# Moving one operand of VectorE's bit operations into PSUM, and lo parts to GpSimd, in the first group of a chain of attention and two expert layers

## The chip, the cores and the metric

One Trainium2 chip, one core of it. The metric is the device time of one execution in microseconds (us). Five engines work side by side: TensorE (PE, with its weight loads as PEld), VectorE (DVE), ScalarE (ACT), GpSimd (POOL) and SyncE (SP), which only issues transfers here.

## What is computed

```python
def _attn_ref(q, k, v, g_norm):                       # 4 x 8 x 576 x 64
    kv = np.einsum('bhsd,bhse->bhde', k, v)
    out = np.einsum('bhsd,bhde->bhse', q, kv)
    rms = np.sqrt(np.mean(out * out, axis=-1, keepdims=True) + 1e-06)
    return (out / rms * g_norm).astype(np.float32)

def _moe_ref(x, w_in, w_out):                         # 2304 x 512, d_ff 2048
    h = x @ w_in
    relu6 = np.clip(h + 3.0, 0.0, 6.0)
    g = h * relu6 / 6.0
    return (g @ w_out).astype(np.float32)
```

A third layer sends each of the 2304 tokens to one of 8 experts (softmax gate, a capacity of 576 per expert), with two products and a ReLU, and weights the result by the gate. `w_in` and `w_out` come as float64, all else as float32.

## The kernel before

TensorE multiplies in float16. Every float32 operand x is split into a hi part, float16(x), and a lo part, float16(x - hi), and a product is three matmuls: hi by hi, hi by lo, lo by hi (`PAIRS`). The float64 weights are first turned into float32 by bit operations on their two 32-bit words.

The 2304 tokens are worked in five groups of 512 (the last has 256). For a group, `mm1` makes 16 blocks of h (f = 0 to 15, twelve matmuls of 512 columns each), `gated` turns each block of h into hi and lo of g, and `mm2` sums g by `w_out` into four PSUM banks. The attention of a batch of 576 tokens, which makes the group's input `x0T`, runs between. The experts come last, with weights that are loaded and split meanwhile.

What matters here is the first group, where the weights are converted while they are first used. It is written out by hand, in program order on every engine (`early`, a manual schedule):

- `load_kv(0)`, `gn` (two transfers for `g_norm`), `load_q(0)`, three pieces of `w_in`, `load_kv(1)` and `wg_raw` (the gate's weights, L150) are issued on SyncE's one queue in this order. L178 (ScalarE) and L179 (VectorE) make hi and lo of `wg`; their place in the engines' order is the scheduler's.
- `first_group` makes q times kv for 512 tokens into four PSUM banks `o`, squares them on ScalarE, copies them to SBUF on VectorE (`oc`, L347), sums the squares by a matmul (`ss`), and makes 1/rms by a square root, a reciprocal and one Newton step (L361 to L366). A matmul by `back` spreads it over the rows (`spread`); `norm` multiplies (L383) and copies the hi part on ScalarE (L384); `low` subtracts for the lo part (L388).
- `f64_piece` converts a piece of 128 x 1024 weights: three bit operations on VectorE (L228, L231, L234), two scaled copies on ScalarE (L239 the hi part, L241 the float32 in place), and the lo part on GpSimd (L243). `convert(i, 3)` runs three of these steps. At every even f the loop runs the three VectorE steps of the piece two ahead, then the other three of the next piece. There are 8 pieces of `w_in` and 8 of `w_out`; the second product's loop goes on in the same manner with pieces 10 to 15. A raw piece has one of three buffers, and `feed` issues the next load behind L234.
- `gated` has L570 (ScalarE), L572 (VectorE, one operand from SBUF and one from PSUM), L574 (ScalarE) and L575, the lo part, on GpSimd, but on VectorE for every fourth f.
- `att_o(1, (3, 1, 1))` makes the attention rows of batch 1 inside the second product's loop, 3, 1 and 1 blocks at a time: squares (L429), sums (L430), the norm (L435 to L452), the product (L458), then `hand_over` (hi L470 on ScalarE, lo L472 on GpSimd, a transposing DMA into x0T). Its `row` tiles have two buffers.

PSUM has eight banks: `psb` holds seven tiles of one bank, `pss` one tile for the gate (`lg`, `pos`, `cp`). `warm` issues matmuls whose result nobody reads.

```python
            eng.tensor_tensor(out=gt[:, 1, :n_t], in0=g6, in1=gt[:, 0, :n_t], op=ALU.subtract)   # L575
...
            gated(0, f, hs[f], nc.vector if f % 4 == 3 else nc.gpsimd)                           # L659
```

Of the kernel before, what the change touches and what calls it, by code (L numbers as in the profile page):

```python
# [30 lines left out]
def moe_chain(ctx: ExitStack, tc: tile.TileContext, qT, k, v, g_norm, w_in, w_out,  # L31
# [150 lines left out]
    nc.vector.tensor_scalar(out=gn, in0=gn, scalar1=S_WIN, scalar2=None, op0=ALU.mult)  # L182
# [88 lines left out]
    with ExitStack() as p1:  # L271
        psb = p1.enter_context(tc.tile_pool(name="psb", bufs=7, space=bass.MemoryType.PSUM))
# [7 lines left out]

        x0T = {}
# [6 lines left out]
        def att_kv(b):  # L288
# [28 lines left out]
        def first_group(w_a, w_b):  # L317
# [16 lines left out]
            nc.vector.tensor_scalar(out=back, in0=head, scalar1=mine, scalar2=None, op0=ALU.is_equal)  # L334
# [618 lines left out]
```

## Time and profile before

| | us |
|---|---|
| median of 3 runs | 728.54 (726.21 to 728.97) |
| the profiled execution | 726.38 |
| its span, first to last instruction | 724.6 |
| TensorE busy | 663.7 (92% of the span) |
| VectorE busy | 356.1 (49%) |
| ScalarE busy | 276.4 (38%) |
| GpSimd busy | 112.2 (15%) |
| mean granted TensorE clock | 0.966 |

The profile counts an instruction as busy from its start to its end, a wait for a shared resource inside it too. An instruction's row has its start, its duration, its line, its tiles (out<-in), its shape, and in brackets the idle time of its engine before it with what ended it. The group of the expert layer is the longest part; the first group ends when the second group's first matmul starts.

### The profile page before, as it was taken

To read this page: it belongs to the slowest core of one execution; us is meant where nothing else is said; L and a number is where in the kernel's file an instruction comes from. 1 tells how busy PE (TensorE), PEld (TensorE's weight loads), DVE (VectorE), ACT (ScalarE), POOL (GpSimd) and SP (SyncE) were. 2 spreads that over 40 slices of the span, in tenths; PEclk is the share of its full clock that TensorE was granted. 3 is DMA by queue.
4 is the path that set the end of the run, shared out by engine and by line. 5 is a ranking of instruction groups with operands and counts; after the bars stand their busy time and mean duration, and the time that the engine had idled before them with its cause. 6 is when DMAs were issued, how large, how long until landed. Compare 5 with 4: busy or idle time off the path is not lost. (4 is left out here: it accounts for less than half of the span.)

```text
span 724.6 us, 12556 instructions
## 1 busy us (share of the span) xinstructions
PE 663.7 (92%) x5049; PEld 378.7 (52%) x5049; DVE 356.1 (49%) x790; ACT 276.4 (38%) x428; POOL 112.2 (15%) x107
## 2 busy tenths in 40 slices
PE   7876969699989999999999999988999999996995
PEld 3332424244454444554444448655776776674754
DVE  1888875745666145461465027552124661163353
ACT  1356553334552035530254007431134551254252
POOL 1145653440100010000000001001111011000101
PEclk7899998989999999999999999999999999998999
DMA  8869669543164760634100015618819995099650
GB/s 307 281 204 280 186 184 350 172 121 118 51 154 83 214 210 19 232 61 107 44 31 1 14 44 133 174 31 132 218 39 298 287 235 161 31 266 195 208 104 23
DMA packets 125221, 108.78 MB, mean 150 GB/s; under 512 B 83943, under 2 KB 88551, under 8 KB 125152
## 3 DMA queue, kind: packets, MB, share of 16 engines
q1 hardware_dynamic: 122096, 98.42, 50.9%
q0 software_dynamic: 3056, 9.41, 3.8%
q8 instruction: 47, 0.77, 0.5%
q14 instruction: 22, 0.18, 0.1%
HBM read 64.55 MB, written 25.23 MB: 124 GB/s over the span
## 5 line engine op out<-in xcount | busy, mean ns | idle before, releaser
L590 PE MATMUL x<-w,g 128*128 128x512 f16 x864 | 197.5, 388 | 14.0 <-POOL w L243 10.6
L562 PE MATMUL h<-x0T,w 128*128 128x512 f16 (+1 forms) x960 | 196.8, 363 | 12.5 <-POOL w L243 10.6
L562 PEld LDWEIGHTS <-w 128*128 128x128 f16 x960 | 92.4, 99 | 106.9 <-POOL w L243 13.0
L590 PEld LDWEIGHTS <-g 128*128 128x128 f16 x864 | 84.5, 99 | 117.2 <-issue 24.4
L849 PE MATMUL h<-xe,w 128*128 128x128 f16 (+1 forms) x1920 | 109.3, 220 | 13.2 <-PEq L887 5.3
L849 PEld LDWEIGHTS <-w 128*128 128x128 f16 x1920 | 106.9, 100 | 20.1 <-issue 14.5
L864 PE MATMUL y<-w,ht 128*128 128x512 f16 (+1 forms) x504 | 112.3, 379 | 1.6 <-DVE ht L773 1.6
L864 PEld LDWEIGHTS <-ht 128*128 128x128 f16 (+1 forms) x504 | 48.9, 99 | 55.7 <-issue 1.7
L854 DVE SCALAR_TENSOR_TENSOR ht<-h,ht 128x512 f16<-128x512 f32 (+1 forms) x40 | 26.5, 663 | 93.0 <-ACT ht L853 89.4
L572 DVE SCALAR_TENSOR_TENSOR g<-t,h 128x512 f32<-128x512 f32 (+1 forms) x80 | 50.1, 630 | 39.4 <-ACT t L570 39.4
L574 ACT ACTIVATE g<-g 128x512 f16<-128x512 f32 (+1 forms) x80 | 46.2, 584 | 54.5 <-DVE g L572 54.2
L570 ACT ACTIVATE t<-h,b 128x512 f32<-128x512 f32 (+1 forms) x80 | 51.2, 641 | 37.6 <-PE h L562 37.5
L543 POOL DMA_INDIRECT xd<-row,sl x18 | 19.6, 1091 | 283.2 <-DVE sl L541 162.1
L575 DVE TENSOR_TENSOR g<-g,g 128x512 f16<-128x512 f32 (+1 forms) x68 | 42.1, 627 | 29.7 <-ACT g L574 29.7
L259 DVE SCALAR_TENSOR_TENSOR w<-raw_kv,w 128x1024 f16<-128x1024 f32 x33 | 40.1, 1220 | 32.1 <-ACT w L256 31.2
L875 POOL DMA_INDIRECT out<-ysb,ti x21 | 21.2, 1011 | 208.3 <-ACT ysb L874 87.4
L597 DVE SCALAR_TENSOR_TENSOR row<-x,row 128x512 f16<-128x512 f32 x18 | 12.3, 690 | 75.6 <-ACT row L596 75.6
L243 POOL TENSOR_TENSOR w<-f,w 128x1024 f16<-128x1024 f32 x16 | 40.3, 2516 | 55.9 <-ACT f L241 55.6
L853 ACT ACTIVATE ht<-h 128x512 f16<-128x512 f32 (+1 forms) x40 | 23.0, 576 | 64.6 <-PE h L849 45.7
L874 ACT ACTIVATE ysb<-y,meta 128x512 f32<-128x512 f32 (+1 forms) x21 | 14.4, 687 | 76.4 <-PE y L864 55.7
L596 ACT ACTIVATE row<-x 128x512 f16<-128x512 f32 x18 | 10.8, 597 | 76.5 <-PE x L590 37.8
L256 ACT ACTIVATE w<-raw_kv 128x1024 f16<-128x1024 f32 x33 | 34.4, 1047 | 0.9 <-ACTq L887 0.8
(121 smaller groups left out, 474.3 us busy)
## 6 DMA issues: line engine op xcount, KB each, us to landing
raw_kv<-in_w SPq DMA_DIRECT2D x33, 512.0 KB, 6.2
xd<-zero SPq DMA_DIRECT2D x20, 514.0 KB, 8.1
raw_w<-in_w SPq DMA_DIRECT2D x19, 512.0 KB, 6.9
raw_w<-in_w_in SPq DMA_DIRECT2D x8, 1024.0 KB, 5.9
raw_w<-in_w_out SPq DMA_DIRECT2D x8, 1024.0 KB, 9.9
raw_q<-in_w SPq DMA_DIRECT2D x12, 512.0 KB, 5.2
raw_q<-in_qT SPq DMA_DIRECT2D x8, 576.0 KB, 5.8
out<-zero SPq DMA_DIRECT2D x6, 768.0 KB, 4.0
```

What stands on the lines that cost most here:

```text
L243: nc.gpsimd.tensor_tensor(out=d[:, 1], in0=f32, in1=d[:, 0], op=ALU.subtract)
L256: nc.scalar.activation(d[:, :, 0, :], r, AF.Copy, scale=scale)
L259: nc.vector.scalar_tensor_tensor(out=d[:, :, 1, :], in0=r, scalar=scale, in1=d[:, :, 0, :], op0=ALU.mult, op1=ALU.subtract)
L562: nc.tensor.matmul(ps, w[:, a, c * 256 + o : c * 256 + o + P], x0T[g][:, b * NP + c, :n_t], start=start and n == 0, stop=stop and n == len ...
L570: nc.scalar.activation(t, ps, AF.Relu, bias=b3, scale=sc / (S_X0 * S_WIN))
L572: nc.vector.scalar_tensor_tensor(out=g6, in0=t, scalar=6.0 * sc, in1=ps, op0=ALU.min, op1=ALU.mult)
L574: nc.scalar.activation(gt[:, 0, :n_t], g6, AF.Copy)
L575: eng.tensor_tensor(out=gt[:, 1, :n_t], in0=g6, in1=gt[:, 0, :n_t], op=ALU.subtract)
L590: nc.tensor.matmul(ps, gts[g][f][:, a, j * P : (j + 1) * P], w[:, b, o : o + DM], start=(f == 0 and i == 0), stop=(f == NF - 1 and i == le ...
L849: nc.tensor.matmul(ps[:, f, :ns], w[c // 2][:, c % 2, a, f * P : (f + 1) * P], xe[:, b * NP + c, :ns], start=(n == 0), stop=(n == 3 * NP - 1))
L854: nc.vector.scalar_tensor_tensor(out=ht[:, 1, :, :ns], in0=ps[:, :, :ns], scalar=0.0, in1=ht[:, 0, :, :ns], op0=ALU.max, op1=ALU.subtract)
L864: nc.tensor.matmul(ps[:ns], hts[q][:, a, f, :ns], w[f // 2][:, f % 2, b, :], start=(n == 0), stop=(n == 3 * NFE - 1))
```

## The change

- The bit operations keep their intermediate `u` in PSUM (L228 and L231 write it, L231 and L234 read it): a tile of two banks, which the gate's `lg`, `pos` and `cp` now share. `psb` has six banks.
- In the norm, the products with `ms` are kept in the second half of the bank `ss`; the factor -0.5 goes into `back`.
- The copies `oc` of q times kv go from VectorE to ScalarE, behind the square root and the first piece's two copies. The first piece's three bit operations stand ahead of the norm.
- `gated` of the first group sends every lo part to GpSimd, and `low(3)` goes there too. The pieces 1 and 2 are converted behind all of `norm`.
- Eight warm-up matmuls go between the second and the third chunk of `att_kv(0)`, fourteen more ahead of the sixteen behind the norm. `load_q(0)` is issued ahead of `gn`.
- `att_o(1)` works in parts of (2, 1, 1, 1), from f = 4 on.

```diff
     load_kv(0)
+    load_q(0)
     gn = const.tile([P, 1], F32, name="gn")
...
-    load_q(0)
...
+            u = two_banks("u").bitcast(I32).rearrange("p (c n) -> p c n", c=c)
             t = cvt.tile([P, c, n], I32, tag="f", name="f")
-            nc.vector.tensor_scalar(out=t, in0=r[:, :, :, 1], scalar1=3, scalar2=0x3FFFFFFF,
+            nc.vector.tensor_scalar(out=u, in0=r[:, :, :, 1], scalar1=3, scalar2=0x3FFFFFFF,
                                     op0=ALU.logical_shift_left, op1=ALU.bitwise_and)
             yield
-            nc.vector.scalar_tensor_tensor(out=t, in0=r[:, :, :, 1], scalar=-0x40000000, in1=t,
+            nc.vector.scalar_tensor_tensor(out=u, in0=r[:, :, :, 1], scalar=-0x40000000, in1=u,
                                            op0=ALU.bitwise_and, op1=ALU.bitwise_or)
             yield
-            nc.vector.scalar_tensor_tensor(out=t, in0=r[:, :, :, 0], scalar=29, in1=t,
+            nc.vector.scalar_tensor_tensor(out=t, in0=r[:, :, :, 0], scalar=29, in1=u,
                                            op0=ALU.logical_shift_right, op1=ALU.bitwise_or)
...
-        psb = p1.enter_context(tc.tile_pool(name="psb", bufs=7, space=bass.MemoryType.PSUM))
+        psb = p1.enter_context(tc.tile_pool(name="psb", bufs=6, space=bass.MemoryType.PSUM))
...
+        def two_banks(name):
+            return pss.tile([P, 1024], F32, tag="s", name=name)
...
+                if pause and c == 2:
+                    pause()
...
-            nc.vector.tensor_scalar(out=back, in0=head, scalar1=mine, scalar2=None, op0=ALU.is_equal)
+            nc.vector.tensor_scalar(out=back, in0=head, scalar1=mine, scalar2=-0.5 * S_X0,
+                                    op0=ALU.is_equal, op1=ALU.mult)
...
-                oc = sg.tile([P, T], F32, tag="g", name="oc")
-                nc.vector.tensor_copy(oc, ps)
-                banks.append(oc)
+                banks.append(ps)
...
-                if p:
-                    next(w_a)
+            for _ in range(3):
+                next(w_a)
...
+            for p in range(NP):
+                oc = sg.tile([P, T], F32, tag="g", name="oc")
+                nc.scalar.activation(oc, banks[p], AF.Copy)
+                banks[p] = oc
...
-            nc.vector.tensor_tensor(out=u, in0=r, in1=r, op=ALU.mult)
-            nc.vector.scalar_tensor_tensor(out=u, in0=u, scalar=-0.5 * S_X0, in1=ms, op0=ALU.mult, op1=ALU.mult)
-            nc.vector.scalar_tensor_tensor(out=r, in0=u, scalar=1.5 * S_X0, in1=r, op0=ALU.add, op1=ALU.mult)
+            nc.vector.tensor_tensor(out=q, in0=r, in1=ms, op=ALU.mult)
+            nc.vector.tensor_tensor(out=q, in0=r, in1=q, op=ALU.mult)
+            nc.vector.scalar_tensor_tensor(out=r, in0=q, scalar=-3.0, in1=r, op0=ALU.add, op1=ALU.mult)
+            warm(14)
             warm(16)
...
-            next(w_b)
             x3 = norm(3)
             low(2, x2, nc.vector)
-            low(3, x3, nc.vector)
-            next(w_b)
-            next(w_b)
+            low(3, x3, nc.gpsimd)
+            for _ in range(3):
+                next(w_b)
...
-        warm(11)
-        keep_kv(att_kv(0))
+        wb = bank("warm")
+        warm(11, wb)
+        keep_kv(att_kv(0, lambda: warm(8, wb)))
...
-            gated(0, f, hs[f], nc.vector if f % 4 == 3 else nc.gpsimd)
+            gated(0, f, hs[f], nc.gpsimd)
...
-        att1 = att_o(1, (3, 1, 1))
+        att1 = att_o(1, (2, 1, 1, 1))
...
-            if 5 <= f <= 11:
+            if 4 <= f <= 11:
                 next(att1)
```

The order moves at three places that matter. ScalarE ahead of the first group's first matmul: `w` and `f` are a weight piece, `x0T` the group's input, `wg` the gate's weights. Before:

```order
L358 ACTIVATE rms<-ss,eps 128x256
L239 ACTIVATE w<-f,gn 128x1024
L241 ACTIVATE f<-f,gn 128x1024
L384 ACTIVATE x0T<-xn 128x512 x4
L178 ACTIVATE wg<-wg_raw 128x4x8
L239 ACTIVATE w<-f,gn 128x1024
```

and now:

```order
L363 ACTIVATE rms<-ss,eps 128x256
L239 ACTIVATE w<-f,gn 128x1024
L241 ACTIVATE f<-f,gn 128x1024
L368 ACTIVATE oc<-o 128x512 x4
L178 ACTIVATE wg<-wg_raw 128x4x8
L395 ACTIVATE x0T<-xn 128x512 x4
L239 ACTIVATE w<-f,gn 128x1024
```

The four `oc` copies came in, and L178 went from behind the four copies into x0T to ahead of them.

VectorE in the norm, up to the second tile. Before:

```order
L361 TENSOR_SCALAR rms<-ss 128x256
L363 RECIPROCAL rms<-rms 128x256
L364 TENSOR_TENSOR rms<-rms 128x256
L365 SCALAR_TENSOR_TENSOR rms<-rms 128x256
L366 SCALAR_TENSOR_TENSOR rms<-rms 128x256
L383 TENSOR_TENSOR xn<-oc,r 128x256 x4
L388 TENSOR_TENSOR x0T<-xn,x0T 128x512
```

and now:

```order
L371 TENSOR_SCALAR ss<-ss 128x256
L372 RECIPROCAL rms<-rms 128x256
L374 TENSOR_TENSOR ss<-rms,ss 128x256
L375 TENSOR_TENSOR ss<-rms,ss 128x256
L376 SCALAR_TENSOR_TENSOR rms<-ss,rms 128x256
L394 TENSOR_TENSOR xn<-oc,r 128x256 x2
L179 SCALAR_TENSOR_TENSOR wg<-wg_raw,wg 128x4x8
L394 TENSOR_TENSOR xn<-oc,r 128x256 x2
L399 TENSOR_TENSOR x0T<-xn,x0T 128x512
```

The products write `ss`, which is in PSUM, and L179 stands between the first and the second tile.

GpSimd in the first product's rounds (L243 a weight piece, L575 the lo part of g). Before:

```order
L243 TENSOR_TENSOR w<-f,w 128x1024
L575 TENSOR_TENSOR g<-g_415,g 128x512
L243 TENSOR_TENSOR w<-f,w 128x1024
L575 TENSOR_TENSOR g<-g_464,g 128x512
L575 TENSOR_TENSOR g<-g_484,g 128x512
```

and now:

```order
L243 TENSOR_TENSOR w<-f,w 128x1024
L585 TENSOR_TENSOR g<-g_442,g 128x512
L585 TENSOR_TENSOR g<-g_462,g 128x512
L243 TENSOR_TENSOR w<-f,w 128x1024
L585 TENSOR_TENSOR g<-g_492,g 128x512
L585 TENSOR_TENSOR g<-g_512,g 128x512
```

Every round has two lo parts there; before it was two and one in turn.

## Rows read from the trace of the kernel before

**Rows 1.** Busy us (x instructions) by stretch, then clock, DMA share, GB/s
```profile
core 0: us, PE busy (x) PEld busy (x) DVE busy (x) ACT busy (x) POOL busy (x), PEclk, DMA share, GB/s
31.80:164.05 132.25, 105.05 (x514) 47.60 (x513) 95.26 (x108) 63.26 (x86) 64.20 (x36) 0.90 0.69 208
164.05:724.60 560.55, 534.94 (x4391) 318.74 (x4389) 246.95 (x657) 205.41 (x332) 42.89 (x54) 0.99 0.50 126
```

**Rows 2.** TensorE in order of time: start, us, what, [idle before, releaser]
```profile
109.99 13.10 PE L590 MATMUL x<-w,g 128*128 128x512 f16 x47 [3.76 <-POOL w L243]
...
141.09 0.38 PE L590 MATMUL x<-w,g 128*128 128x512 f16 x1 [3.07 <-ACT w L239]
144.38 4.85 PE L590 MATMUL x<-w,g 128*128 128x512 f16 x11 [2.91 <-POOL w L243]
...
164.05 20.88 PE L562 MATMUL h<-x0T,w 128*128 128x512 f16 x96
```

**Rows 3.** VectorE and ScalarE in one round of the first product
```profile
60.66 0.67 ACT L570 ACTIVATE t<-h,b 128x512 f32<-128x512 f32 x1
...
61.37 0.69 DVE L572 SCALAR_TENSOR_TENSOR g<-t,h 128x512 f32<-128x512 f32 x1 [1.27 <-ACT t L570]
...
62.63 1.13 ACT L239 ACTIVATE w<-f,gn 128x1024 f16<-128x1024 f32 x1
62.70 1.22 DVE L231 SCALAR_TENSOR_TENSOR f<-raw_w,f 128x1024 int32<-128x1024 int32 x1
...
63.85 1.15 ACT L241 ACTIVATE f<-f,gn 128x1024 f32<-128x1024 f32 x1
63.95 2.06 DVE L234 SCALAR_TENSOR_TENSOR f<-raw_w,f 128x1024 int32<-128x1024 int32 x1
64.91 0.67 ACT L570 ACTIVATE t<-h,b 128x512 f32<-128x512 f32 x1
...
65.94 0.67 DVE L572 SCALAR_TENSOR_TENSOR g<-t,h 128x512 f32<-128x512 f32 x1
...
67.96 0.69 DVE L572 SCALAR_TENSOR_TENSOR g<-t,h 128x512 f32<-128x512 f32 x1 [1.34 <-ACT t L570]
```

**Rows 4.** VectorE's groups from 40 to 97 us: busy us, mean ns | idle
```profile
L234 DVE SCALAR_TENSOR_TENSOR f<-raw_w,f 128x1024 int32<-128x1024 int32 x8 | 19.5, 2442 | 0.3
...
L572 DVE SCALAR_TENSOR_TENSOR g<-t,h 128x512 f32<-128x512 f32 x15 | 10.2, 681 | 9.1 <-ACT t L570 9.1
L228 DVE TENSOR_SCALAR f<-raw_w 128x1024 int32<-128x1024 int32 x7 | 5.3, 757 | 0.0
L575 DVE TENSOR_TENSOR g<-g,g 128x512 f16<-128x512 f32 x3 | 2.1, 692 | 2.1 <-ACT g L574 2.1
```

**Rows 5.** VectorE beside GpSimd, in order of time
```profile
26.18 2.12 POOL L243 TENSOR_TENSOR w<-f,w 128x1024 f16<-128x1024 f32 x1 [22.29 <-ACT f L241]
26.22 2.36 DVE L365 SCALAR_TENSOR_TENSOR rms<-rms 128x256 f32<-128x256 f32 x1
...
41.06 2.66 POOL L243 TENSOR_TENSOR w<-f,w 128x1024 f16<-128x1024 f32 x1 [7.43 <-ACT f L241]
41.66 0.68 DVE L572 SCALAR_TENSOR_TENSOR g<-t,h 128x512 f32<-128x512 f32 x1
```

**Rows 6.** ScalarE's L570 of f = 2 and of f = 14
```profile
47.84 0.69 ACT L570 ACTIVATE t<-h,b 128x512 f32<-128x512 f32 x1 [0.65 <-PE h L562]
...
95.66 0.67 ACT L570 ACTIVATE t<-h,b 128x512 f32<-128x512 f32 x1
```

**Rows 7.** The transfers of the microsecond from 27 to 28
```profile
DMA packets 542, 0.19 MB, mean 188 GB/s; under 512 B 457, under 2 KB 457, under 8 KB 542
```

**Rows 8.** The first copy into x0T, and the third matmul of f = 2
```profile
31.11 1.29 ACT L384 ACTIVATE x0T<-xn 128x512 f16<-128x512 f32 x2 [5.01 <-DVE xn L383]
...
43.78 1.71 PE L562 MATMUL h<-x0T,w 128*128 128x512 f16 x4 [3.32 <-POOL w L243]
```

**Rows 9.** The second group's x after its q products, and the products' release
```profile
217.71 26.07 PE L590 MATMUL x<-w,g 128*128 128x512 f16 x120
...
220.89 1.29 DVE L458 TENSOR_TENSOR xs<-o,r 128x512 f32<-128x512 f32 x2
```

More of the change, by code (lines that the diff above doesn't have):

```diff
@@ L181, in moe_chain @@
     xd = dram.tile([E * CAPP, ROW], F16, name="xd")
-    nc.vector.tensor_scalar(out=gn, in0=gn, scalar1=S_WIN, scalar2=None, op0=ALU.mult)
     steps = []
@@ L286, in group_tile, with att_kv @@
             return x0T[g]
-        def att_kv(b):
+        def att_kv(b, pause=None):
             ps = bank("kv").rearrange("p (a b) -> p a b", b=P)
@@ L338, in first_group @@
             banks = []
-            ss = bank("ss")[:, : T // 2]
             sqs = []
@@ L345, in first_group @@
                 nc.scalar.activation(sq, ps, AF.Square)
-                oc = sg.tile([P, T], F32, tag="g", name="oc")
-                nc.vector.tensor_copy(oc, ps)
-                banks.append(oc)
+                banks.append(ps)
                 sqs.append(sq)
-                if p:
-                    next(w_a)
+            for _ in range(3):
+                next(w_a)
+            ss = bank("ss")
             for p, sq in enumerate(sqs):
                 for i, rows in enumerate(halves):
-                    nc.tensor.matmul(ss[rows, :], sel[:, p, :], sq[:, i * T // 2 : (i + 1) * T // 2],
+                    nc.tensor.matmul(ss[rows, : T // 2], sel[:, p, :], sq[:, i * T // 2 : (i + 1) * T // 2],
                                      start=p == 0, stop=p == NP - 1)
-            small = [sg.tile([P, 2, T // 2], F32, tag="g", name="rms") for _ in range(2)]
-            ms, r, u = small[0][:, 0], small[0][:, 1], small[1][:, 0]
-            nc.scalar.activation(u, ss, AF.Sqrt, bias=eps, scale=1.0 / D)
+            ms, q = ss[:, : T // 2], ss[:, T // 2 :]
+            r = sg.tile([P, T // 2], F32, tag="g", name="rms")
+            u = sg.tile([P, T // 2], F32, tag="g", name="rms")
+            nc.scalar.activation(u, ms, AF.Sqrt, bias=eps, scale=1.0 / D)
             next(w_a)
             next(w_a)
-            nc.vector.tensor_scalar(out=ms, in0=ss, scalar1=1.0 / D, scalar2=1.0e-6, op0=ALU.mult, op1=ALU.add)
+            for p in range(NP):
+                oc = sg.tile([P, T], F32, tag="g", name="oc")
+                nc.scalar.activation(oc, banks[p], AF.Copy)
+                banks[p] = oc
             next(w_a)
+            nc.vector.tensor_scalar(out=ms, in0=ms, scalar1=1.0 / D, scalar2=1.0e-6, op0=ALU.mult, op1=ALU.add)
             nc.vector.reciprocal(r, u)
-            nc.vector.tensor_tensor(out=u, in0=r, in1=r, op=ALU.mult)
-            nc.vector.scalar_tensor_tensor(out=u, in0=u, scalar=-0.5 * S_X0, in1=ms, op0=ALU.mult, op1=ALU.mult)
-            nc.vector.scalar_tensor_tensor(out=r, in0=u, scalar=1.5 * S_X0, in1=r, op0=ALU.add, op1=ALU.mult)
+            nc.vector.tensor_tensor(out=q, in0=r, in1=ms, op=ALU.mult)
+            nc.vector.tensor_tensor(out=q, in0=r, in1=q, op=ALU.mult)
+            nc.vector.scalar_tensor_tensor(out=r, in0=q, scalar=-3.0, in1=r, op0=ALU.add, op1=ALU.mult)
+            warm(14)
             warm(16)
@@ L487, in gate_block @@
                 nc.sync.dma_start_transpose(xT, row[:, : 2 * DM])
-            lg = pss.tile([P, P], F32, tag="s", name="lg")
+            lg = two_banks("lg")
             for a in range(2):
@@ L504, in gate_block @@
             yield
-            pos = pss.tile([P, P], F32, tag="s", name="pos")
+            pos = two_banks("pos")
             nc.tensor.matmul(pos[:, :E], upper, oh, start=True, stop=False)
@@ L602, in moe_chain @@
         for i in range(NS):
-            w, c = f64_piece(("i", i), gn)
+            w, c = f64_piece(("i", i), gn, two_banks)
             win.append(w)
@@ L606, in moe_chain @@
         for i in range(NS):
-            w, c = f64_piece(("o", i), S_WOUT)
+            w, c = f64_piece(("o", i), S_WOUT, two_banks)
             wout.append(w)
@@ L629, in moe_chain, with warm @@
         early.enter_context(tc.manual_schedule())
-        def warm(n):
-            ps = bank("warm")
+        def warm(n, ps=None):
+            ps = bank("warm") if ps is None else ps
             for _ in range(n):
@@ L637, in moe_chain @@
         next(start)
-        warm(11)
-        keep_kv(att_kv(0))
+        wb = bank("warm")
+        warm(11, wb)
+        keep_kv(att_kv(0, lambda: warm(8, wb)))
+        nc.vector.tensor_scalar(out=gn, in0=gn, scalar1=S_WIN, scalar2=None, op0=ALU.mult)
         hs = next(start)
@@ L734, in moe_chain @@
         mm2(ps, g, 0, range(4, 6))
-        cp = pss.tile([P, P], F32, tag="s", name="cp")
+        cp = two_banks("cp")
         nc.tensor.matmul(cp[:, :E], ones, total, start=True, stop=True)
```

2 lines of the change are left out of this document (1 added, 1 removed).

## The prediction

> **What bounds the kernel now.** I read the busy time by stretch first [rows 1], then TensorE's order of time [rows 2], one round of the first group on VectorE and ScalarE [rows 3], and last the rows that price single steps. The stretches split the run in two. From 164.05 us on TensorE works 534.94 of 560.55 us: it is the bound, and nothing that the change does to other engines shows there. Before that, from the first group's first matmul at 31.80 us, it works 105.05 of 132.25 us at a mean granted clock of 0.90, while VectorE works 95.26: the 27.2 us that TensorE stands idle are what the change can reach. The order of time names whom TensorE waits for: GpSimd's lo part of a weight piece (L243), or the ScalarE copy before it (L239) [rows 2].
>
> A round of the group's first product handles two f. VectorE's and ScalarE's rows hang on each other [rows 3]: VectorE's L572 (61.37), then ScalarE's L239 (62.63), L241 (63.85), L570 (64.91), and on VectorE's side L228, L231 (62.70) and L234 (63.95) before the next L572 (65.94) and the one behind it (67.96). The reader is to see L234: 2.06 us, where L231 of the same shape took 1.22. Over the stretch L234 means 2442 ns [rows 4]. The cause shows at 26 us: GpSimd's L243 ran from 26.18 to 28.30, and VectorE's L365, which has a quarter of L231's elements, took 2.36 us from 26.22 on: it ended just behind L243 [rows 5]. But L572, with one operand from PSUM, ran 0.68 us at 41.66, inside an L243 that lasted from 41.06 to 43.72 [rows 5]. So it is two SBUF operands on VectorE that collide with GpSimd, and the change puts one of them in PSUM.
>
> **The rounds of the first product.** Six rounds lie between the L570 of f = 2 (47.84) and that of f = 14 (95.66) [rows 6]: 47.82 / 6 = 7.97 us each. What is the round without collisions?
> - By ScalarE [rows 3]: from L572 at 61.37 to L239 1.26, to L241 1.22, to L570 1.06, from an L570 to its L572 0.71 (60.66 to 61.37), and from one L572 of a pair to the other 2.02: 6.27 us.
> - By VectorE: from L572 to L231 1.33 (62.70 - 61.37), to L234 1.25, L234 itself 1.22, and 2.02: 5.82, to which the dearer L228 is added. No row has a VectorE write into PSUM. L228 is bounded below by the 0.69 that it takes undisturbed (757 ns on the mean [rows 4]) and above by twice L231, 2.44. I take 1.22: with an operand in PSUM it becomes like L572 and L231, which pass one element a cycle (512 in 0.68, 1024 in 1.22). That adds 0.53: 6.35 us.
> - By GpSimd: an L243, which took 2.66 at its longest in rows 5, and two L575 of half its elements are about 5.3.
> - By TensorE: 24 matmuls at 20.88 / 96 = 0.2175 [rows 2] are 5.2 us.
>
> VectorE's 6.35 ends last, just ahead of ScalarE. The gain is 7.97 - 6.35 = 1.62 a round, **9.7 us** over six. The 692 ns of L575 that leave VectorE in every second round [rows 4] are in it. If L228 stayed at 0.69, ScalarE's 6.27 would set the round and the gain be 10.2; if it took 2.44, the round would be 7.57 and the gain 2.4.
>
> [...]
>
> **The start.** The change takes four copies off VectorE, frees L365 from its 2.36 us, keeps TensorE at work before the third chunk of `att_kv` and lets q go ahead of `g_norm`. My reckoning has the norm ready some 4 us sooner, the 30 warm-up matmuls done at about 24.9, and VectorE's first normalised tile ready at 26.7. But ScalarE's queue now has L178 (`wg`) ahead of the four copies into x0T, where it stood behind them, and L179 stands on VectorE ahead of the second tile. `wg_raw` is loaded behind nearly everything else of the start, and the same bytes lie before it as now. Its 512 packets of 32 bytes pass between 27 and 28 us: 457 small ones in that microsecond [rows 7]. So L178 can't run before 28; I take 29.7, between that and 31.11, where the copies start now [rows 8]. The first copy into x0T then moves from 31.11 to 29.9 only: **1.2 us**. From there to the third matmul of f = 2 (43.78) it is 12.67 us now [rows 8]; GpSimd takes one lo part off VectorE (0.69) and L243 takes 2.12 instead of 2.66 (0.54), the late L179 costs 0.35: about 0.9 more. Conversion 2 and two round trips on VectorE end 0.6 us behind that, so I count **1.5 us** at the L570 of f = 2. Bounds: nothing, if `wg_raw` lands at 31; 4.5, if it lands before 26.7.
>
> **Between the two products.** From 95.66 to the second matmul of f = 2 of the second product (109.99) it is 14.33 us. L243 of that piece falls from about 2.66 to 2.12 (0.5), and the last pair of f, cleared of its collision, is shorter by 0.6: **1.1 us**. TensorE's idle time there (3.76) [rows 2] stays.
>
> **The second product, 109.99 to 164.05.** It loses 3.07 us to L239 and 2.91 to L243 near 141 [rows 2]: `att_o(1)`'s first part has three rows where there are two row buffers, the third waits for a transposing DMA, and the conversion stands behind it on ScalarE. Parts of (2, 1, 1, 1) don't need a third. Behind the gap 11 matmuls take 4.85 us, 0.44 each where 0.2175 is the full rate: 2.4 more. Together 8.4. Laying the queues out anew, piece by piece, I get short waits instead, at f = 8, 10, 12 and 14, of which 0.6 is net new: **7.8 us**. Between nothing, if the new waits are as long, and 10.
>
> **The sum.** 1.5 + 9.7 + 1.1 + 7.8 = 20.1 us. Behind 164.05 every engine's order is unchanged and TensorE is the bound, so all of it should reach the end. The bank that is taken from `psb` I cost at nothing: the second block of a later group would take the first q product's bank, given back at 222.2 (220.89 + 1.29), and it starts 48 matmuls, 10.4 us, behind 217.71 [rows 9]; without that cover it would cost some 3 us in each of two groups. From the profiled execution's 726.38 us (724.6 of it span) that leaves 706.3. The median of the runs is 728.54, 2.2 above; I say 707.0, between 706.3 and 708.4.
>
> **Rivals.**
> - GpSimd and VectorE still exclude each other, so the change doesn't do what it says. For it: no row shows a VectorE write to PSUM. Against it: L572 at 41.66 [rows 5]. L575 leaves VectorE and the parts of `att_o(1)` still help: 1.5 + 4 + 0.5 + 4 = 10 us, some **716 us**. A lost bank that does cost 6 us comes out near it, at 712. Chance 0.18.
> - `wg_raw` lands before ScalarE comes to L178. Against it: the packets at 27 us [rows 7]. The start then gains 3 us more: **703.5 us**. Chance 0.13.
> - Slower: VectorE's writes into PSUM are slow. The round tips past 7.97 when L228 and L231 need over 2.03 us each (6.35 + 2 x 0.81). At 2.44 the round is 8.8: six rounds lose 5 us, two conversions in the start 2.4 each, and the second product keeps no gain: 726.4 + 5 + 4.8 - 2.6 (start and tail), some **734 us**. [...] Chance 0.03.
>
> **How the numbers follow.** The forecast has 0.64, 702 to 711; with 0.18, 0.13 and 0.03 that leaves 0.02 for no change (waits that only move, 725 to 730). The range 699 to 717 takes in the second rival whole and most of the first. A measurement of this kernel tells about 0.5% from no change, 3.6 us: faster 0.95, same 0.02, slower 0.03.
>
> **What would show it.** L228 and L234 near 1.22 in the rounds, L243 at 2.1 to 2.2 throughout; L580 (L570 before) every two f at 6.3 us; L178 on ScalarE waiting for a DMA until about 29.7, with TensorE idle before its first h; no gap of 3 us in the middle of the second product; group 1's first matmul (L572 in the changed file) near 144 instead of 164. I am wrong if L234 stays above 2, if L228 exceeds 1.5, or if TensorE loses over 2 us anew behind 144.

## The result and the profile after

The changed kernel takes 702.88 us (median of 4 runs, 701.10 to 704.98) where the kernel before, in runs beside it, takes 727.38 (4 runs, 725.21 to 728.97): a ratio of 0.967, with a 95% interval of 0.962 to 0.971. The profiled execution took 701.10 us, its span 699.3; before they were 726.38 and 724.6. The forecast was 707.0, and the gain between the profiled executions is 25.3 us where the sum had 20.1. That the two are near each other hides two misses: the first group gave 17.8 us, less than its terms, and 7.5 us came from behind it, where I had said that nothing changes.

The same two stretches as in [rows 1], cut at the first h of the first and of the second group (the second group's first matmul slipped ahead to 139.83; 146.23 is its second, at 146.45, less the 0.22 of one matmul):

```profile
core 0: us, PE busy (x) PEld busy (x) DVE busy (x) ACT busy (x) POOL busy (x), PEclk, DMA share, GB/s
31.19:146.23 115.04, 99.84 (x512) 46.27 (x512) 83.00 (x108) 62.87 (x86) 59.67 (x41) 0.94 0.82 241
146.23:699.30 553.07, 532.77 (x4391) 316.83 (x4389) 247.19 (x657) 205.81 (x332) 42.55 (x54) 1.00 0.50 128
```

The first stretch is 17.2 us shorter than its counterpart, with VectorE busy for 12.3 us less; it begins 0.6 us earlier. The second, with the same number of matmuls, fell from 560.55 to 553.07.

TensorE in order of time, against [rows 2, 8]:

```profile
31.19 0.38 PE L572 MATMUL h<-x0T,w 128*128 128x512 f16 x1 [3.35 <-ACT x0T L395]
...
42.44 12.24 PE L572 MATMUL h<-x0T,w 128*128 128x512 f16 x48 [2.78 <-POOL w L243]
...
98.60 10.55 PE L600 MATMUL x<-w,g 128*128 128x512 f16 x35 [2.99 <-POOL w L243]
...
120.12 2.53 PE L600 MATMUL x<-w,g 128*128 128x512 f16 x11 [0.31 <-POOL w L243]
...
127.82 2.53 PE L600 MATMUL x<-w,g 128*128 128x512 f16 x11 [1.23 <-POOL w L243]
...
134.66 5.34 PE L600 MATMUL x<-w,g 128*128 128x512 f16 x24 [0.61 <-POOL w L243]
...
141.49 5.12 PE L600 MATMUL x<-w,g 128*128 128x512 f16 x23 [1.27 <-POOL w L243]
146.45 20.67 PE L572 MATMUL h<-x0T,w 128*128 128x512 f16 x95
```

The gap of 3 us in the middle of the second product is gone; four waits on L243 stand in its place (0.31, 1.23, 0.61 and 1.27).

One round of the first product, VectorE and ScalarE, against [rows 3]:

```profile
59.75 0.67 ACT L580 ACTIVATE t<-h,b 128x512 f32<-128x512 f32 x1
...
60.52 0.69 DVE L582 SCALAR_TENSOR_TENSOR g<-t,h 128x512 f32<-128x512 f32 x1
...
62.55 0.69 DVE L582 SCALAR_TENSOR_TENSOR g<-t,h 128x512 f32<-128x512 f32 x1 [1.34 <-ACT t L580]
63.16 1.22 DVE L228 TENSOR_SCALAR u<-raw_w 128x1024 int32<-128x1024 int32 x1
...
65.69 1.23 DVE L234 SCALAR_TENSOR_TENSOR f<-raw_w,u 128x1024 int32<-128x1024 int32 x1
66.09 0.67 ACT L580 ACTIVATE t<-h,b 128x512 f32<-128x512 f32 x1
```

L234 takes 1.23 us where it took 2.06, and the round, from one L580 to the next but one, 6.34. The groups from 40 to 97 us, VectorE's and then GpSimd's, against [rows 4]:

```profile
L231 DVE SCALAR_TENSOR_TENSOR u<-raw_w,u 128x1024 int32<-128x1024 int32 x9 | 11.1, 1232 | 0.3
L234 DVE SCALAR_TENSOR_TENSOR f<-raw_w,u 128x1024 int32<-128x1024 int32 x9 | 11.0, 1223 | 0.4
L582 DVE SCALAR_TENSOR_TENSOR g<-t,h 128x512 f32<-128x512 f32 x16 | 11.0, 687 | 11.2 <-ACT t L580 11.2
L228 DVE TENSOR_SCALAR u<-raw_w 128x1024 int32<-128x1024 int32 x8 | 9.8, 1220 | 0.0
...
L243 POOL TENSOR_TENSOR w<-f,w 128x1024 f16<-128x1024 f32 x9 | 19.2, 2136 | 14.0 <-ACT f L241 14.0
```

### The profile page after: what moved, and what is told of

It reads as the page before. It is cut to its first block, busy times and chain, and to the rows that moved or that the text cites. A ratio compares the mean times of both kernels' runs of the same rounds, so it can differ in the third digit from the quotient of the medians.

```text
span 699.3 us, 12621 instructions
## 1 busy us (share of the span) xinstructions
PE 656.1 (94%) x5071; PEld 374.9 (54%) x5071; DVE 340.3 (49%) x786; ACT 278.4 (40%) x433; POOL 107.3 (15%) x112
## 5 line engine op out<-in xcount | busy, mean ns | idle before, releaser
L600 PE MATMUL x<-w,g 128*128 128x512 f16 x864 | 194.1, 383 | 8.7 <-POOL w L243 6.4
L572 PEld LDWEIGHTS <-w 128*128 128x128 f16 x960 | 92.3, 98 | 102.9 <-issue 9.0
L861 PE MATMUL h<-xe,w 128*128 128x128 f16 (+1 forms) x1920 | 107.2, 218 | 8.6 <-PEq L899 3.1
L861 PEld LDWEIGHTS <-w 128*128 128x128 f16 x1920 | 104.9, 99 | 15.2 <-issue 9.8
L580 ACT ACTIVATE t<-h,b 128x512 f32<-128x512 f32 (+1 forms) x80 | 51.2, 640 | 36.7 <-PE h L572 36.5
L584 ACT ACTIVATE g<-g 128x512 f16<-128x512 f32 (+1 forms) x80 | 46.2, 585 | 45.7 <-DVE g L582 45.4
L259 DVE SCALAR_TENSOR_TENSOR w<-raw_kv,w 128x1024 f16<-128x1024 f32 x33 | 40.2, 1223 | 32.1 <-ACT w L256 31.5
L585 DVE TENSOR_TENSOR g<-g,g 128x512 f16<-128x512 f32 (+1 forms) x64 | 39.4, 623 | 27.0 <-ACT g L584 26.9
L887 POOL DMA_INDIRECT out<-ysb,ti x21 | 21.2, 1008 | 202.6 <-ACT ysb L886 85.8
L607 DVE SCALAR_TENSOR_TENSOR row<-x,row 128x512 f16<-128x512 f32 x18 | 12.3, 690 | 74.2 <-ACT row L606 74.2
L243 POOL TENSOR_TENSOR w<-f,w 128x1024 f16<-128x1024 f32 x16 | 34.1, 2132 | 39.1 <-ACT f L241 39.1
```

The lines of the kernel that those rows point to most:

```text
L243: nc.gpsimd.tensor_tensor(out=d[:, 1], in0=f32, in1=d[:, 0], op=ALU.subtract)
L259: nc.vector.scalar_tensor_tensor(out=d[:, :, 1, :], in0=r, scalar=scale, in1=d[:, :, 0, :], op0=ALU.mult, op1=ALU.subtract)
L572: nc.tensor.matmul(ps, w[:, a, c * 256 + o : c * 256 + o + P], x0T[g][:, b * NP + c, :n_t], start=start and n == 0, stop=stop and n == len ...
L580: nc.scalar.activation(t, ps, AF.Relu, bias=b3, scale=sc / (S_X0 * S_WIN))
L584: nc.scalar.activation(gt[:, 0, :n_t], g6, AF.Copy)
L600: nc.tensor.matmul(ps, gts[g][f][:, a, j * P : (j + 1) * P], w[:, b, o : o + DM], start=(f == 0 and i == 0), stop=(f == NF - 1 and i == le ...
```

## The experiments

Each is a change to one of the two kernels. The table puts the profiled executions beside each other: the start of ScalarE's first step of f = 2, the mean of the six rounds from there to f = 14, TensorE's start with the second piece of the second product (its second matmul), group 1's first h, and the experts, from the block that waits for `xe` to the end of the span. The last column is the ratio of the runs to the kernel before, run beside them, with its 95% interval.

| kernel | f = 2 | round | second product | group 1's h | experts | ratio |
|---|---|---|---|---|---|---|
| before | 47.84 | 7.97 | 109.99 | 164.05 | 227.99 | 1 |
| changed | 46.96 | 6.42 | 98.60 | 146.23 | 221.84 | 0.967 (0.962 to 0.971) |
| e1 | 48.44 | 7.90 | 110.16 | 159.83 | 228.19 | 0.994 (0.991 to 0.997) |
| e2 | 48.33 | 7.17 | 104.60 | 152.62 | 225.95 | 0.980 (0.975 to 0.984) |
| e3 | 47.72 | 7.89 | 109.27 | 160.16 | 222.01 | 0.982 (0.978 to 0.986) |
| e4 | 47.65 | 6.96 | 102.68 | 150.43 | 220.54 | 0.972 (0.969 to 0.976) |
| e5 | 48.13 | 7.98 | 110.33 | 164.24 | 221.81 | 0.991 (0.989 to 0.993) |
| e6 | 46.99 | 6.41 | 98.60 | 146.22 | 227.63 | 0.978 (0.976 to 0.980) |
| e7 | 45.08 | 6.48 | 97.81 | 145.16 | 223.04 | 0.962 (0.959 to 0.964) |
| e8 | 43.17 | 6.67 | 95.67 | 143.70 | 222.81 | 0.965 (0.963 to 0.967) |
| e9 | 47.34 | 6.41 | 98.94 | 145.66 | 221.16 | 0.968 (0.965 to 0.972) |
| e10 | 42.52 | 6.54 | 91.32 | 147.40 | 222.02 | 0.970 (0.966 to 0.974) |
| e11 | 43.92 | 6.54 | 92.71 | 148.84 | 220.04 | 0.971 (0.968 to 0.975) |
| e12 | 42.73 | 6.48 | 95.45 | 143.21 | 220.12 | 0.963 (0.960 to 0.965) |

**e1, the attention's parts alone.** Before, with:

```diff
-        att1 = att_o(1, (3, 1, 1))
+        att1 = att_o(1, (2, 1, 1, 1))
-            if 5 <= f <= 11:
+            if 4 <= f <= 11:
```

> The kernel before with batch 1's attention in parts of (2, 1, 1, 1) from f = 4 on, nothing else; seven banks, the intermediate in SBUF. Theory (the second product's gap came from the third row, which waits for a row buffer): the two waits near 141 us (3.07 and 2.91) and the slow matmuls behind them go, short waits of 0.5 to 1.5 us come: the stretch from the second product's second piece to group 1's first h falls from 54.1 by 3 to 5 us, the rounds stay at 7.97 us, total 4 us under the kernel before (0.993 to 0.996). Rival (the gap came from conversions slowed by GpSimd): the stretch falls by less than 1 us, total the same.

722.80 us (7 runs). The second product falls from 54.06 to 49.67 us, 4.4, and the rounds stay: the theory. (The new parts are no free choice: with six banks, four of them `acc`, a part of three rows would have no bank for its third.)

**e2, the intermediate in PSUM, on top of e1.** The change's lines in `f64_piece`, `two_banks` and the pools, nothing else:

```diff
-        psb = p1.enter_context(tc.tile_pool(name="psb", bufs=7, space=bass.MemoryType.PSUM))
+        psb = p1.enter_context(tc.tile_pool(name="psb", bufs=6, space=bass.MemoryType.PSUM))
...
+            u = two_banks("u").bitcast(I32).rearrange("p (c n) -> p c n", c=c)
...
-            nc.vector.tensor_scalar(out=t, in0=r[:, :, :, 1], scalar1=3, scalar2=0x3FFFFFFF,
+            nc.vector.tensor_scalar(out=u, in0=r[:, :, :, 1], scalar1=3, scalar2=0x3FFFFFFF,
```

> The kernel before with the intermediate u in PSUM (two banks, psb six) and the parts of (2, 1, 1, 1) that six banks need; norm, oc copies, lo parts and q's load as before. Theory (two SBUF operands on VectorE collide with GpSimd; one in PSUM ends it): L234 1.22 us, L228 1.22, L243 2.13 throughout; a round 6.6 to 7.2 us instead of 7.97 (VectorE still has a lo part in every second round); first h still near 31.8; total 12 to 15 us under the kernel before (0.979 to 0.984). Rival (the lo parts and the order free VectorE, not PSUM): L234 stays above 1.8 and the total is within 2 us of the run with the parts alone. For the banks: no wait over 1 us at group 1's x behind its q products.

712.15 us (4 runs). L234 (L235 in that file) means 1224 ns, L228 also 1224, the round 7.17, and group 1's h comes 7.2 us before that of e1. The rival falls: PSUM frees VectorE without any lo part moved. (Both kernels with the operand in SBUF also write L231 and L234 over what they read. That this isn't the cause L228 shows: it doesn't do so, and GpSimd held it too, 2.62 us instead of 0.69, as rows in the next section show.) Behind the q products (200.32, for 4.75 us) the second group's x follow at once, at 205.01, so the lost bank costs nothing.

**e3, the changed kernel with the intermediate in SBUF.**

```diff
-            u = two_banks("u").bitcast(I32).rearrange("p (c n) -> p c n", c=c)
             t = cvt.tile([P, c, n], I32, tag="f", name="f")
+            u = t
```

> The changed kernel with the bit operations' intermediate back in SBUF (L228 writes t, L231 and L234 work in it), all else as changed. Theory: L234 above 2 us on the mean, L243 2.5 to 2.9, L228 back at 0.7 to 0.8; a round 7.6 to 8.6 us instead of 6.37; total 8 to 14 us over the changed kernel (711 to 717). Rival (lo parts on GpSimd and the new order are what freed the round): within 2 us of 703.

715.13 us (4 runs). VectorE's groups of this run from 40 to 97 us:

```profile
L234 DVE SCALAR_TENSOR_TENSOR f<-raw_w,f 128x1024 int32<-128x1024 int32 x8 | 18.7, 2333 | 0.3
L231 DVE SCALAR_TENSOR_TENSOR f<-raw_w,f 128x1024 int32<-128x1024 int32 x8 | 12.3, 1539 | 0.3
L582 DVE SCALAR_TENSOR_TENSOR g<-t,h 128x512 f32<-128x512 f32 x15 | 10.2, 682 | 10.9 <-ACT t L580 9.0 <-POOL g L585 1.9
L228 DVE TENSOR_SCALAR f<-raw_w 128x1024 int32<-128x1024 int32 x7 | 6.1, 877 | 0.0
```

The collision is back, on L231 and L228 as well, and the round is 7.89: with all lo parts on GpSimd, but the operand in SBUF, next to nothing of the 7.97 is gained. PSUM alone gives 0.73 a round (7.90 to 7.17), the lo parts alone nothing that counts, both together 1.55. Here more work for GpSimd paid only once PSUM had freed VectorE.

**e4, every fourth lo part back on VectorE.**

```diff
-            gated(0, f, hs[f], nc.gpsimd)
+            gated(0, f, hs[f], nc.vector if f % 4 == 3 else nc.gpsimd)
```

> The changed kernel with every fourth lo part of the first group's g (f = 3, 7, 11, 15) back on VectorE. Theory (VectorE sets the round, and the lo part there waits for ScalarE's L584 with the next piece's L228 queued behind it): every second round is 1.0 to 1.5 us longer, 3 to 5 us in all, total 706 to 708. Rival (VectorE has 1.3 us idle in each round, the lo part fits in it): under 1 us, the same.

706.95 us (4 runs); the six rounds are 3.3 us longer, group 1's h 4.2 later. The lo part costs more than its 0.69 us: at 65.91 in its trace it starts after a wait of 0.70 for ScalarE's L584, and the next piece's L228 stands behind it.

**e5 and e6, the code's place.** Where the 7.5 us behind the first group come from, the two traces show among the experts. TensorE, before and then after, at the block behind `xe`, at the only jumps from one expert to another that cost over 1 us of "issue" time, and at the last block:

```profile
496.61 7.15 PE L849 MATMUL h<-xe,w 128*128 128x128 f16 x96 [2.50 <-DMA xe<-xd]
...
657.03 0.89 PE L849 MATMUL h<-xe,w 128*128 128x128 f16 x13 [3.11 <-PEq L887]
661.30 6.66 PE L849 MATMUL h<-xe,w 128*128 128x128 f16 x83 [3.39 <-issue]
...
707.70 5.53 PE L849 MATMUL h<-xe,w 128*128 128x128 f16 x96 [2.05 <-DVEq L887]
```

```profile
477.46 5.52 PE L861 MATMUL h<-xe,w 128*128 128x128 f16 x96 [1.82 <-DMA xe<-xd]
...
539.34 1.50 PE L861 MATMUL h<-xe,w 128*128 128x128 f16 x24 [0.81 <-PEq L899]
542.42 4.19 PE L861 MATMUL h<-xe,w 128*128 128x128 f16 x72 [1.59 <-issue]
...
635.41 5.52 PE L861 MATMUL h<-xe,w 128*128 128x128 f16 x96 [0.73 <-PEq L899]
...
680.78 7.16 PE L861 MATMUL h<-xe,w 128*128 128x128 f16 x96 [2.05 <-DVEq L899]
```

L887 (L899 now) is the branch that leaves out an expert's blocks for which there are no tokens. Before, at the sixth expert, TensorE waits 3.11 us at the jump, does 13 matmuls, and waits 3.39 for nothing that the profile shows; after the change that jump costs 0.73, and the third expert's has a wait 24 matmuls behind it. The waits for PEq and "issue" at the jumps fall from 8.7 to 4.7 us together. The 83 matmuls behind the long wait took 6.66 us, at a granted clock of 0.50 from 658.5 to 665 us, where 83 of 96 in 5.52 are 4.8: 1.9 more. (The block of 7.15 us behind `xe`, before, and the last one of 7.16, after, cancel.) e1 and e2 have the long wait where before has it, e3 and e4 the short one where the changed kernel does. What tells the two kinds apart is how many TensorE instructions lie ahead: the change adds 22 warm-up matmuls with their weight loads. e5 adds such a number to before, e6 takes the 22 from the changed kernel.

```diff
             warm(16)
+            ps = bank("warm")
+            for _ in range(22):
+                nc.tensor.matmul(ps[:, :32], ones, zero[:, :32], start=True, stop=True)
```

> The kernel before with 22 matmuls of 32 columns, whose result nobody reads, behind its 16 warm-up matmuls, in the 3.02 us in which TensorE waits for the norm: the same 44 TensorE instructions (with the weight loads) that the change's 22 warm-up matmuls add ahead of the experts, and nothing else. Theory (the stall of 3.11 + 3.39 us at a jump between two experts, at 654 to 661 us, comes from where the code of TensorE lies): it goes, and one of 2 to 2.5 us comes at the first jump, 97 us earlier, where the changed kernel has it (24 matmuls behind the jump, not 13); the stretch from group 1's first h to the end falls from 560.5 by 4 to 7 us, total 0.990 to 0.995 of the kernel before; up to 164 us within 0.7 us of it. Rival (a chance of transfers, or a consequence of the earlier first group): the stall stays at the later jump, total within 1 us.

719.11 us (6 runs), 6.7 us below the kernel before in its runs, by matmuls that compute nothing. TensorE there:

```profile
559.36 1.50 PE L852 MATMUL h<-xe,w 128*128 128x128 f16 x24 [0.81 <-PEq L890]
561.88 4.19 PE L852 MATMUL h<-xe,w 128*128 128x128 f16 x72 [1.03 <-issue]
...
655.07 5.52 PE L852 MATMUL h<-xe,w 128*128 128x128 f16 x96 [0.73 <-PEq L890]
```

The wait stands 24 matmuls behind the third expert's jump, as foreseen, and the experts fell from 227.99 to 221.81. e6 is the changed kernel with:

```diff
-            warm(14)
...
-        keep_kv(att_kv(0, lambda: warm(8, wb)))
+        keep_kv(att_kv(0))
```

> The changed kernel without its 22 further warm-up matmuls (8 in the attention's first product, 14 behind the norm). Theory of the code's place: the stall of 5 to 7 us at the later jump between experts is back (13 matmuls behind it), the one of 2.4 us at the first jump goes: 3 to 6 us more behind group 1's first h. Theory of the start (ScalarE waits for the gate's small transfer until 30.4 us anyway): q times kv runs at the lower clock, 6.7 us instead of 3.7, the norm is ready later by up to 3 us, and the first h moves by under 0.7 us only. Total 3 to 6 us over the changed kernel (706 to 709). Rival of the first: no change behind the first group. Rival of the second: the first h 2 to 3 us later.

710.02 us (5 runs), more than the 706 to 709 expected. TensorE at the sixth expert:

```profile
640.91 1.06 PE L860 MATMUL h<-xe,w 128*128 128x128 f16 x13 [3.11 <-PEq L898]
645.18 6.28 PE L860 MATMUL h<-xe,w 128*128 128x128 f16 x83 [3.21 <-issue]
```

Both theories hold: the wait is back with its 13 matmuls, and group 1's first h (146.22) does not move. In this kernel, where the gate's transfer sets the start, the 22 warm-up matmuls give nothing to the first group; all that they give is where the experts' code lies. (The rest of the loss: a wait for a row's transposing DMA at 190 us took 2.37 us instead of 1.33, and TensorE ran slower behind it, at a mean granted clock of 0.79 from 188 to 196 us instead of 1.00.)

That the code comes in from outside while the program runs is what I read in a row of the page's part on the DMA queues. Of the kernel before:

```profile
q8 instruction: 47, 0.77, 0.5%
```

47 packets, 0.77 MB: 16.4 KB each, on a queue that the page calls instruction, beside the experts' weights and the other transfers, which keep the DMA engines 72% busy from 496.61 us to the end of the run before. That the waits are for such packets, and that they hold code, is not shown. What the runs show is that 44 more TensorE instructions ahead take the wait of 3.39 us from 13 matmuls behind the sixth expert's jump and put one of 1.03 (e5) 24 matmuls behind the third's, and that without the 22 warm-up matmuls it is back at the sixth (3.21, e6). How many instructions a packet holds was not shown either, so where else a wait falls can't be worked out from it.

**e7, the gate's weights later.** The changed kernel, with L178 and L179 moved behind the last h of the first product (the second of them moves in the same way):

```diff
-    nc.scalar.activation(wg[:, :, :E], wg_raw, AF.Copy, scale=S_GATE)
...
+        nc.scalar.activation(wg[:, :, :E], wg_raw, AF.Copy, scale=S_GATE)
...
         list(att_o(0, (1,), T))
```

> The changed kernel with the two instructions that make the gate's weights (L178 on ScalarE, L179 on VectorE) moved from ahead of the first group's first copy to behind its last h. Theory (ScalarE's queue stands 5.1 us for a transfer of 16 KB in small packets): the first copy into x0T moves from 30.5 to 27.9 us, and with it the conversions, f = 2 and every round: group 1's first h 2 to 3 us earlier, total 699.5 to 701 (0.996 of the changed kernel). Rival (the second piece's conversion or its load is late next): the first h is earlier, f = 2 by under 1 us, total within 1 us of the changed kernel.

698.20 us (6 runs, 696.27 to 701.66; the profiled one is the slowest). In the changed kernel ScalarE stood as I had said:

```profile
30.39 0.23 ACT L178 ACTIVATE wg<-wg_raw 128x32 f16<-128x32 f32 x1 [5.11 <-DMA wg_raw<-in_w_gate]
30.53 0.61 ACT L395 ACTIVATE x0T<-xn 128x512 f16<-128x512 f32 x1
```

Moved, the first copy starts at 28.89 (27.21 in e8, where the norm was earlier), f = 2 is 1.9 us earlier than in the changed kernel, and 1.1 of it reach group 1's h in the profiled execution. The rival (under 1 us at f = 2) falls, though the 2 to 3 us at group 1's h are not reached in this execution; on the median the run is 3 to 5 us below those of the changed kernel (701.41 in e9, 702.88).

**e8 and e10, another order of the round.** VectorE, ScalarE and TensorE work 5.05, 4.9 and 5.2 us of a round's 6.4, so I tried twice to let them overlap more. e8, on top of e7, with a hook `between` in `gated` ahead of the copy to hi, and one step fewer to do at the start of the second product:

```diff
+            if f == 0:
+                convert(1, 1)
             if f % 2 == 0:
-                convert(kf + 2, 3)
-                convert(kf + 1, 3)
+                convert(kf + 2, 2)
...
+            if f % 2 == 0:
+                gated(0, f, hs[f], nc.gpsimd, lambda: convert(kf + 1, 2))
+                convert(kf + 2, 1)
+            else:
+                gated(0, f, hs[f], nc.gpsimd, lambda: convert(kf + 2, 1))
```

> The run with the gate's weights moved, and besides the rounds of the first product in another order on ScalarE and VectorE: the two scaled copies of a piece stand between gated's first and second ScalarE step (L580, L239 or L241, L584), the third bit operation behind the first L582, so that ScalarE works while VectorE makes L582. Theory (a round of 6.37 us is ScalarE's chain, 4.9 us of work and two waits of 0.75 for L582, with VectorE at 5.05 and TensorE at 5.2): a round of 5.2 to 5.6, 5 to 8 us under the run with the gate's weights moved. Rival (VectorE's order, where each L582 now stands behind a bit operation, or the buffers of six banks): a round of 6 us or more, under 3 us.

699.79 us (5 runs), the plain round 6.42 where the changed kernel has 6.34: the theory failed. ScalarE and TensorE of this run:

```profile
49.59 0.69 ACT L577 ACTIVATE t<-h,b 128x512 f32<-128x512 f32 x1 [1.64 <-PE h L569]
```

```profile
47.16 5.35 PE L569 MATMUL h<-x0T,w 128*128 128x512 f16 x24 [1.06 <-POOL w L240]
```

TensorE waits for the piece, whose lo part waits for the copy that I had put behind a step that waits for TensorE. e10 undoes this loop; against e7, with the same hook, and without the steps at the start of the second product that are then done already:

```diff
+            if f == 0:
+                convert(1, 3)
             if f % 2 == 0:
                 convert(kf + 2, 3)
-                convert(kf + 1, 3)
...
-            gated(0, f, hs[f], nc.gpsimd)
+            gated(0, f, hs[f], nc.gpsimd, lambda: convert(kf + 2, 1 + f % 2))
```

> The rounds again, on top of the moved gate's weights, without the loop that the last order made (TensorE's h, L580, L241, L243 on GpSimd, TensorE's next h: 2.6 + 0.7 + 1.15 + 2.13 = 6.6 us): now all three bit operations of a piece stand ahead of the round, L239 between L580 and L584 of the even f, L241 between those of the odd f, and L243 behind it, a round ahead of the matmuls that need it. Theory (ScalarE's 4.9 us of work, its waits filled; TensorE at 5.2 is the next bound): a round of 5.2 to 5.7, six rounds 31 to 34 us, group 1's first h 4 to 7 us earlier than with the gate's weights moved alone, total 692 to 696. Rival (the loads of the raw pieces or VectorE's order hold the round at 6 or more): under 2 us.

703.11 us (6 runs): failed too. There the plain round is 6.72, and the loop runs between two engines: the hi copy (L236 in that file) waits 2.35 for VectorE's third bit operation, and VectorE's second L579 waits 1.78 for the ScalarE step that stands behind that copy. It comes to the second product's second piece 6.5 us before e7 (91.32, 97.81), and loses that and 2.2 us more up to group 1's h: the wait of 3 us for L240 comes at the third piece (101.69), and another of 2.91 at 127.97, behind a row that waited 4.98 us for its buffer where it waited 3.41 in e7. The round thus looks like a chain through four engines' queues: no engine is full, and neither order shortened it.

**e9, e11, e12, the code's place once more.** e9 is the changed kernel again, beside e10 and e11. e11 builds on e10, e12 on e7; the last argument is the number of columns, and both have 120 more instructions ahead of the experts than the changed kernel (the number was my estimate of a place without a wait, which no run before these two shows):

```diff
-        keep_kv(att_kv(0, lambda: warm(8, wb)))
+        keep_kv(att_kv(0, lambda: warm(68, wb, 32)))
```

```diff
-            warm(14)
+            warm(74, None, 32)
```

> The changed kernel once more, beside the two runs that build on it. Both theories: 701 to 705; group 1's first h near 146, the stall between experts at the first jump, 24 matmuls behind it, not at the later one.

> The same, with 68 matmuls of 32 columns in place of the 8 warm-up matmuls of the attention's first product: 120 more TensorE instructions ahead of the experts. [...]

> The run with the gate's weights moved (e7), and 74 matmuls of 32 columns in place of the 14 warm-up matmuls behind the norm: 120 more TensorE instructions ahead of the experts than in the changed kernel, 2.0 us of them (0.027 each, as 68 took 1.86) where 14 took 3.2. Theory of the code's place: no stall by issue at any jump between experts, each jump 0.7 to 0.9; the experts 1.5 to 3 us shorter than the 221.2 to 223.0 of the runs with the changed kernel's place. Theory of the start: the spread of the norm waited for the warm-ups, the first h comes 0.5 to 1 us earlier than in e7. Total 695 to 697, 0.956 to 0.960 of the kernel before. Rival: the fewer full matmuls lower the clock in the first rounds, and the total is that of e7 (0.962).

e9: 701.41 us (6 runs), group 1's h at 145.66 and the wait 24 matmuls behind the third expert's jump, as expected. e11: 704.80 (6 runs). e12: 699.16 (6 runs). TensorE at the third and the sixth expert in e12:

```profile
540.96 5.52 PE L861 MATMUL h<-xe,w 128*128 128x128 f16 x96 [0.80 <-PEq L899]
...
635.41 5.52 PE L861 MATMUL h<-xe,w 128*128 128x128 f16 x96 [0.74 <-PEq L899]
```

The jumps for PEq cost 0.73 to 0.88 us and have no wait for "issue" behind them any more, in e11 and in e12: this part of e12's expectation held. Its total did not, nor did its start: the first h comes 2.4 us before e7's (27.21, 29.57) where 0.5 to 1 was said. e11's median lies 1.7 us above e10's, and its first h comes 1.4 us after (29.09, 27.73); e8 and e10, with e7's start, have it at 27.89 and 27.73, so most of that isn't the warm-up matmuls. e12's total is the one that its rival named, but the rounds, 6.48 as in e7, don't bear out the rival's reason. In e12 the experts took 1.0 us less than in e9 (though their first block took 7.15 us instead of 5.52). In e11 and e12 the row's DMA in group 1 was waited for longer (1.90 and 2.13 us, 0.95 in e7), and the six matmuls behind it took 2.13 and 2.44 us, 1.46 in e7 (in e12 the granted clock was 0.79 from 186 to 194 us, as in e6): from its first h to its x group 1 took 54.7 and 55.1 us, where e7 took 52.3. So e12 begins group 1 2.0 us before e7 and comes to its x 0.9 us behind it. What makes that wait long in one run and short in another stays open.

The fastest version is thus e7: its interval (0.9594 to 0.9641) ends just below that of the changed kernel in e9 (0.9645 to 0.9716) and overlaps that of its first runs (0.9621 to 0.9712); e7 and e9 ran on different chips, so how much e7 is ahead is not settled.

## Why the prediction was right, point by point

- **PSUM ends the exclusion.** Right, with the prices: L228 1.22 as chosen between 0.69 and 2.44, L234 1.22, L243 2.14. The six rounds took 38.5 us, 9.3 less (9.7 said); the first of them took 6.45, the next four 6.34, the last 6.69. No dearer read of PSUM shows: L234 with its PSUM operand means 1223 ns, L231 took 1.22 us from SBUF [rows 3]. The rate behind the chosen 1.22 is known only as times: 512 elements in 0.68 us, 1024 in 1.22 [rows 3, 5]. What I didn't see is that the lo parts need PSUM (e3), while PSUM gains without them (e2). And "two SBUF operands on VectorE" was too narrow: L228, which reads one operand from SBUF and writes to SBUF, was held as well. Before:

```profile
107.03 2.91 POOL L243 TENSOR_TENSOR w<-f,w 128x1024 f16<-128x1024 f32 x1 [1.42 <-ACT f L241]
107.88 2.62 DVE L228 TENSOR_SCALAR f<-raw_w 128x1024 int32<-128x1024 int32 x1
```

  It starts inside L243, ends 0.55 us behind it, and takes 2.62 instead of 0.69. Writing its result to PSUM ended that too.
- **The start.** 0.9 us at f = 2 where I had 1.5. The mechanism was right (L178 waits 5.11 us), its end mis-sized: 30.39, not 29.7.
- **Between the products.** From f = 14 to 98.60 it is 13.14 us; 1.2 gained, 1.1 said. But TensorE's idle time there, which was to stay at 3.76, is 2.99: L243 lies in it, and took 2.91 us before (107.03).
- **The second product.** 54.06 to 47.63: 6.4, where I had 7.8. Two sentences failed. "Parts of (2, 1, 1, 1) don't need a third": the second part's row still waits for a row buffer, 2.56 us on ScalarE ahead of the next piece's copy, at 122.90. And the waits that I netted at 0.6 us are 3.4 instead of 0.64. Part of them is the old exclusion where nobody moved the operand: VectorE's mean of the squares (L445, 128x8) beside GpSimd (the first row is the wait for the row buffer):

```profile
122.90 0.63 ACT L480 ACTIVATE row<-xs 128x512 f16<-128x512 f32 x1 [2.56 <-DMA x0T<-row]
...
125.64 2.12 POOL L243 TENSOR_TENSOR w<-f,w 128x1024 f16<-128x1024 f32 x1 [0.88 <-ACT f L241]
126.08 0.68 DVE L440 TENSOR_REDUCE msq<-sq 64x8 f32<-64x512 f32 x1 [0.42 <-ACT sq L439]
126.79 1.00 DVE L445 TENSOR_SCALAR ms<-msq 128x8 f32<-128x8 f32 x1
```

  L445 ends when L243 does (127.79 and 127.76); undisturbed it takes 0.17. It happens in each of the last three parts, 1.7 us in all, in the chain on which the next piece's copies hang.
- **"Behind 164.05 every engine's order is unchanged and TensorE is the bound, so all of it should reach the end."** This step failed. The order is unchanged, the time isn't: 560.55 became 553.07. Of the 7.5 us, 6.2 are the experts (227.99 to 221.84), by the place of their code, which e5 and e6 show in both directions: 4.0 in waits at the jumps and 1.9 in the slower matmuls behind the long one. 0.8 is the shorter wait for a row's DMA in group 1 (1.33 instead of 2.10), and 0.7 the wait for `xe` (1.82 instead of 2.50); I have no cause for these two, and e6 shows that the first can go the other way.
- **The lost bank.** Right, it costs nothing: the q products start at 194.35 and take 4.75 us, and the second group's x start at 199.04.
- **The rivals.** GpSimd and VectorE no longer exclude each other in the bit operations, `wg_raw` didn't land early, and VectorE's writes into PSUM aren't slow (L228 means 1220 ns). Each was read off the row that I had named for it. e3, in which they do exclude each other, came to 715.13, near the 716 of that rival, but by another way: the rounds give 0.5 us where the rival had 4, and the experts' code gives 6.0 that it didn't have.

So the first group gave 17.8 of the 20.1 us, and the total came out beyond them because of an effect that the change brings by accident. That the total lies near the forecast is in that part luck.

## What to carry to other kernels

Where VectorE and GpSimd work side by side, put one of VectorE's two operands into PSUM before giving GpSimd more work: here the lo parts gave 0.08 us a round without the first step (7.97 to 7.89, e3) and 0.75 behind it (7.17 in e2 to 6.42). When an edit adds or takes away instructions ahead of code with branches, compare the stretch behind it in both traces before crediting the edit: here 44 instructions that compute nothing were worth 6 us, a quarter of the gain. A short instruction that waits for a late small transfer belongs behind the work that doesn't need it: here ScalarE's copies into x0T stood behind L178's wait of 5.11 us for `wg_raw`, and with L178 moved f = 2 came 1.9 us earlier (e7).

## What the runs showed of the hardware that I had not expected

- The place of code costs time: a jump to an expert's first block costs 0.73 us, and up to 6.5 (3.11 + 3.39) in the kernel before, where TensorE stopped again 13 matmuls behind the jump's target; with 44 more instructions ahead of it (e5) that jump cost 0.73.
- VectorE's TENSOR_SCALAR of 128x8 elements, with no operand in PSUM, was held until GpSimd's running instruction ended (L445: 0.69, 1.00 and 0.56 us instead of 0.17); a TENSOR_REDUCE of 64x512 that started inside the same GpSimd instruction took its usual 0.68.
- VectorE writes 128x1024 words into PSUM in 1.22 us (L228 after the change), 0.53 slower than the same operation into SBUF undisturbed (0.69) and as fast as its two-operand operations.
- After a wait of 2 to 3 us TensorE's granted clock sometimes falls, and 96 matmuls take 7.15 us instead of 5.52: behind `xe` in before (2.50 us of wait; granted clock 0.50 from 498 to 501 us), but not in e5 (2.62 us of wait, 5.52 for the 96).
